# Four attention steps accumulate their output projection in two borrowed PSUM banks, the last Q products run ahead of one step, and a scratch tile changes its bank

## The chip, the cores and the metric

The kernel runs on one core of a Trainium2 chip. The metric is the device time of one execution in microseconds (us). Each timed execution also lists the mean granted clock of TensorE, the share of full speed that the chip let the matmul engine run at. All executions whose state is on record are "fast", so all may be compared.

Engines are named as the profile names them: PE is TensorE's matmuls, PEld its weight loads, DVE is VectorE, ACT is ScalarE, SPq a DMA queue. Times inside a profile count from the start of the profiled execution.

## The reference

One transformer block on x of shape 1 x 2048 x 1024, in bfloat16: layer normalisation, linear attention with 32 heads, a residual, layer normalisation, a gated MLP of width 3584, a residual.

```python
def _A_ref(x, wqkv, wo):                     # linear attention, 32 heads of 32
    q, k, v = ...                            # from x @ wqkv
    phi = lambda t: jnp.where(t > 0, t + 1, jnp.exp(t)) + 1e-6
    pq, pk = phi(q), phi(k)
    kv = jnp.einsum("bhsd,bhse->bhde", pk, v)
    z = jnp.einsum("bhsd->bhd", pk)
    num = jnp.einsum("bhqd,bhde->bhqe", pq, kv)
    den = jnp.einsum("bhqd,bhd->bhq", pq, z)[..., None] + 1e-6
    o = num / den
    return (...o...) @ wo                    # the output projection
# ... _B_ref: (relu(x @ W_gate) * (x @ W_up)) @ W_down
h = x + _A_ref(_layernorm(x), A_wqkv, A_wo)
h2 = h + _B_ref(_layernorm(h), B_W_gate, B_W_up, B_W_down)
```

## The kernel before

The large products (Q, K, V, gate, up, down) use a scheme of Strassen's kind. It needs sums of sub-blocks of the operands (`left_sums`) and recombines partial products. In the stretch that matters here, three streams share TensorE:

- the last Q products (`q_unit`, profile names Aq, Dq, Eq at line 437),
- the attention steps: numerator and denominator (nd), a DMA transpose (oT), the output projection (attn), and then the residual and second layer normalisation on ScalarE and VectorE,
- the first gate and up products of the MLP (Aq, Dq, Eq at line 693), which need the transposed normalised rows and their sums.

All accumulate in PSUM. In this stretch the pools hold two banks of tag A, two of tag E, one of tag D for the Strassen products, and three of tag ab for the attention steps.

```python
spin = pspool.tile([P, NW], FP32, tag="E", bufs=2, name="spin")   # scratch for matmuls at the very start
...
def nd():                                    # three tiles of tag "ab" in each step
    for c0, n in pieces:
        ps = ndpool.tile([P, NW], FP32, tag="ab", name="nd")
        for c in range(c0, c0 + n):
            nc.tensor.matmul(ps[...], lhsT=pqT[...], rhs=kvz[:, c, :], start=True, stop=True)
        # ... ScalarE: den = ln(...), rd = exp(-den)
        # ... VectorE: o_sb = numerator * rd        -> this frees the bank
def wo_h():                                  # two more tiles of tag "ab" in each step
    for j in range(2):
        ps = abpool.tile([P, NW], FP32, tag="ab", name="attn")
        for c in range(KC):                  # 8 matmuls of 128 x 512
            nc.tensor.matmul(ps[:], lhsT=st["oT"][:, c, :], rhs=wo_sb[...], start=(c == 0), stop=(c == KC - 1))
        nc.vector.scalar_tensor_tensor(...)  # x_res = attn + x_res, frees the bank
    # ... h to DRAM; LayerNorm: two passes over hn on ScalarE and small steps; the transpose of hn follows
...
LAG = (0, 1, 1, 2, 4)                        # nd, oT, x_in, wo_h, hn_T: steps after a tile begins
STS = 8; QSTEPS = 8
for step in range(QSTEPS):                   # steps 0..7: Q products between the attention steps
    attn_step(step)
    ...
    for p in rest[step * len(rest) // QSTEPS:(step + 1) * len(rest) // QSTEPS]:
        next(p)                              # one Q group
# steps 8..11: attention alone, with one gate/up unit; steps 12..19: with gate/up products between them
```

In the traces, a ScalarE or VectorE instruction waits for those queued ahead of it on its engine, even when its own input is ready. An example from the profile before: the step rd at 211.21 us follows a LayerNorm pass that runs from 210.08 to 211.22, though its input den was done at 210.18.

## Time and profile before

The three executions before the prediction took 747.36, 748.55 and 749.38 us; the profiled one took 748.8 us at a granted clock of 0.999.

The first line below is from the summary page of the profile: each engine's busy time (share of the span). The second is from its list of the costliest groups: line, engine, operation, operands, count, then busy us and mean ns, then idle time in front of them.

```profile
PE 725.9 (97%) x4020; PEld 382.2 (51%) x4020; DVE 568.4 (76%) x1023; ACT 324.6 (43%) x596; POOL 5.8 (1%) x44
L536 PE MATMUL attn<-wo_mem,oT 128*128 128x512 bf16 x256 | 57.8, 379 | 3.4 <-DVE o_sb L516 3.1
```

TensorE is the limit. The next view is the busy time of each engine by stretch. Its columns are the stretch, its length, then busy us and instruction count for PE, PEld, DVE, ACT and POOL, then the granted clock, the DMA share and GB/s.

```profile
198.00:230.00 32.00, 25.95 (x143) 12.36 (x142) 27.97 (x82) 22.41 (x66) 0.00 (x0) 1.00 0.71 168
260.00:300.00 40.00, 37.00 (x171) 16.54 (x170) 27.79 (x67) 21.30 (x42) 0.00 (x0) 1.00 0.43 131
300.00:700.00 400.00, 400.00 (x2241) 219.09 (x2239) 309.19 (x478) 128.96 (x172) 0.00 (x0) 1.00 0.64 213
```

From 300 us on PE has no idle time to give. Between 198 and 230 us it idles 6 of 32 us. The list of PE's waits from 185 to 300 us gives what it waited for: total us, number of times, longest. These are its five largest entries.

```profile
PE attn L536 <- DVE o_sb L516: 3.0, 6, 0.9
PE nd L509 <- DVE x_res L538: 1.9, 2, 1.3
PE Aq L693 <- ACT m L153: 1.8, 1, 1.8
PE nd L509 <- DVE pq_mem L201: 1.8, 1, 1.8
PE accA L773 <- DVE gu L702: 0.8, 1, 0.8
```

And these are rows of PE's timeline in that stretch: start, duration, what it is, and in brackets how long PE idled just before and what ended it.

```profile
187.59 3.61 PE L536 MATMUL attn<-wo_mem,oT 128*128 128x512 bf16 x16 [0.40 <-DVE o_sb L516]
...
203.83 0.23 PE L509 MATMUL nd<-kvz,pq_mem 128*128 128x132 bf16 x1 [1.79 <-DVE pq_mem L201]
204.97 3.61 PE L536 MATMUL attn<-wo_mem,oT 128*128 128x512 bf16 x16 [0.90 <-DVE o_sb L516]
...
210.52 3.61 PE L536 MATMUL attn<-wo_mem,oT 128*128 128x512 bf16 x16 [0.43 <-DVE o_sb L516]
...
215.85 3.61 PE L536 MATMUL attn<-wo_mem,oT 128*128 128x512 bf16 x16 [0.39 <-DVE o_sb L516]
...
221.12 0.28 PE L509 MATMUL nd<-kvz,pq_mem 128*128 128x132 bf16 x2 [1.28 <-DVE x_res L538]
222.05 3.61 PE L536 MATMUL attn<-wo_mem,oT 128*128 128x512 bf16 x16 [0.65 <-DVE o_sb L516]
...
262.93 3.62 PE L536 MATMUL attn<-wo_mem,oT 128*128 128x512 bf16 x16
...
297.49 1.02 PE L773 MATMUL accA<-hn,wg 128*128 128x512 bf16 x4 [0.78 <-DVE gu L702]
```

This is one rotation of three ab banks. A step takes five tiles from it, so each product waits until VectorE has emptied the tile of three turns before: projection behind o_sb, num/den behind x_res. The E banks are idle meanwhile: in PE's timeline no E product runs between the last of Q (198.45 us, 0.59 long) and the first of gate and up (232.18). The first row and the last two (the projections of steps 6 and 16, and the first accumulator of the feed-forward part, accA) serve as marks.

### The profile page before, as it was taken

How to read it: one execution, taken by the hardware profiler on the slowest of the kernel's cores; microseconds unless marked ns; L12 is line 12 of the kernel's file. 1: busy time of each engine (PE TensorE's matmuls, PEld its weight loads, DVE VectorE, ACT ScalarE, POOL GpSimd, SP SyncE). 2: the span in 40 equal slices, each digit the busy share in tenths (PEclk: the TensorE clock that was granted, in tenths of full speed). 3: DMA queues.
4: the chain of work that ended last, by engine and by line, in shares of the span. 5: the costliest groups of instructions: out<-in, count | busy, mean ns of one | idle time of the engine just before them, and what ended most of it. 6: DMA issues, size and time to landing. Idle time of an engine off the chain costs nothing.

```text
span 747.0 us, 10654 instructions
## 1 busy us (share of the span) xinstructions
PE 725.9 (97%) x4020; PEld 382.2 (51%) x4020; DVE 568.4 (76%) x1023; ACT 324.6 (43%) x596; POOL 5.8 (1%) x44
## 2 busy tenths in 40 slices
PE   7999999999889999999999999999999999999997
PEld 3444555444344444444444444444444458888666
DVE  6997644777886767678777788877787469996797
ACT  4876554778767645344444344343435220000000
POOL 0000000000000000000000000000000000000000
PEclk9999999999999999999999999999999999999999
DMA  9766002069777525164837349476574399988822
GB/s 317 159 145 154 1 1 94 20 146 249 170 173 172 134 79 183 39 182 121 237 127 207 125 140 317 149 211 212 183 261 149 101 388 361 317 284 299 306 79 79
DMA packets 146580, 132.03 MB, mean 177 GB/s; under 512 B 50913, under 2 KB 128097, under 8 KB 146529
## 3 DMA queue, kind: packets, MB, share of 16 engines
q1 hardware_dynamic: 135392, 123.23, 54.4%
q10 hardware_dynamic: 11136, 8.13, 3.4%
q8 instruction: 31, 0.51, 0.3%
q14 instruction: 21, 0.16, 0.1%
HBM read 79.95 MB, written 39.85 MB: 160 GB/s over the span
## 4 chain that ended last, share of the span: by engine, by line
PE 79%; DVE 8%; ACT 5%; DMA 5%; issue 1%; SPq 0%; POOL 0%; DVEq 0%; ACTq 0%
PE accA L773 22%; PE accY L773 8%; PE accX L773 8%; PE accA L1105 8%; PE attn L536 5%; PE Aq L297 3%; PE accA L934 3%; PE accX L1105 3%; PE Aq L437 3%; PE accY L1105 2%; DMA hn<-hn 2%; PE Aq L693 2%; PE Eq L297 2%; PE accX L934 2%; PE accY L934 2%
## 5 line engine op out<-in xcount | busy, mean ns | idle before, releaser
L783 ACT ACTIVATE gu<-gu 128x512 bf16<-128x512 bf16 x72 | 45.4, 630 | 131.9 <-DVE gu L782 127.4
L778 ACT COPY snap<-accA 128x1024 f32<-128x1024 f32 x72 | 72.4, 1008 | 37.0 <-PE accA L773 36.9
L536 PE MATMUL attn<-wo_mem,oT 128*128 128x512 bf16 x256 | 57.8, 379 | 3.4 <-DVE o_sb L516 3.1
L773 PEld LDWEIGHTS <-tg 128*128 128x128 f16 x384 | 37.6, 98 | 45.3
L773 PEld LDWEIGHTS <-tu 128*128 128x128 f16 x384 | 37.6, 98 | 45.3
L782 DVE TENSOR_TENSOR gu<-accY,snap 128x1024 bf16<-128x1024 f32 x36 | 43.9, 1219 | 9.7 <-ACT snap L778 9.7
L153 ACT COPY u<-Aq 128x512 f32<-128x512 f32 x56 | 32.2, 581 | 43.9 <-PE Aq L297 20.3
L782 DVE TENSOR_TENSOR gu<-accX,snap 128x1024 bf16<-128x1024 f32 x36 | 43.9, 1219 | 7.2 <-PE accX L773 4.7
L773 PE MATMUL accA<-hn,tg 128*128 128x512 f16 (+1 forms) x192 | 49.3, 379 | 0.0
L773 PE MATMUL accA<-hn,tu 128*128 128x512 f16 (+1 forms) x192 | 49.3, 379 | 0.0
L1105 PEld LDWEIGHTS <-x 128*128 128x128 f16 (+1 forms) x448 | 43.8, 98 | 5.5
L773 PEld LDWEIGHTS <-wg 128*128 128x128 bf16 x288 | 28.2, 98 | 34.9 <-issue 1.1
L773 PEld LDWEIGHTS <-wu 128*128 128x128 bf16 x288 | 28.2, 98 | 34.0
L536 PEld LDWEIGHTS <-oT 128*128 128x128 bf16 x256 | 25.0, 97 | 35.0 <-issue 6.7
L786 DVE TENSOR_TENSOR hq<-gu 128x512 bf16<-128x512 bf16 x48 | 20.3, 423 | 14.3 <-ACT gu L783 14.2
L297 PEld LDWEIGHTS <-xT 128*128 128x128 bf16 (+1 forms) x192 | 18.6, 98 | 24.5 <-issue 3.2
L516 DVE TENSOR_TENSOR o_sb<-nd,rd 128x384 bf16<-128x384 f32 (+1 forms) x48 | 22.8, 507 | 8.6 <-ACT rd L515 7.5
L1105 PEld LDWEIGHTS <-xs 128*128 128x128 f16 x280 | 27.4, 98 | 3.2
L538 DVE SCALAR_TENSOR_TENSOR x_res<-attn,x_res 128x512 bf16<-128x512 f32 x32 | 22.0, 688 | 6.3 <-PE attn L536 6.2
L934 PEld LDWEIGHTS <-x 128*128 128x128 bf16 (+1 forms) x168 | 16.5, 98 | 19.6
L1111 DVE TENSOR_TENSOR snap<-accA,u 128x1024 f32<-128x1024 f32 x16 | 19.5, 1220 | 8.3 <-PE accA L1105 8.1
L773 PE MATMUL accA<-hn,wg 128*128 128x512 bf16 x96 | 24.6, 379 | 0.8 <-DVE gu L702 0.8
(232 smaller groups left out, 1415.0 us busy)
## 6 DMA issues: line engine op xcount, KB each, us to landing
x<-x_dram SPq DMA_DIRECT2D x17, 896.0 KB, 8.2
x_dram<-hq SPq DMA_DIRECT2D x28, 512.0 KB, 3.0
wg<-in_B_W_gate_dram SPq DMA_DIRECT2D x14, 512.0 KB, 5.2
wu<-in_B_W_up_dram SPq DMA_DIRECT2D x14, 512.0 KB, 7.4
wraw<-in_B_W_down_dram SPq DMA_DIRECT2D x14, 512.0 KB, 4.9
x_dram<-hq SPq DMA_DIRECT2D x28, 256.0 KB, 2.6
t_dram<-wt SPq DMA_DIRECT2D x28, 256.0 KB, 2.2
xd<-x_dram SPq DMA_DIRECT2D x6, 896.0 KB, 7.2
```

What stands on the lines that cost most here:

```text
L153: nc.scalar.copy(out=snaps[nm, v], in_=A[v][:])
L297: nc.tensor.matmul(ps[:], lhsT=left[m - 1][:, kc, r + v * P:r + (v + 1) * P], rhs=right[m - 1][:, kc, :], start=(start and kc == 0), stop= ...
L437: nc.tensor.matmul(ps[:], lhsT=rq[m - 1][:, kc, (c + v) * P:(c + v + 1) * P], rhs=left[m - 1][:, kc, :], start=(start and kc == 0), stop=( ...
L516: nc.vector.tensor_tensor(out=ov[:, c0:c0 + n], in0=ndv[:, :, 0:P].rearrange("p k (h e) -> p k h e", h=HPC), in1=rd[:, 0:n, :].unsqueeze(3 ...
L536: nc.tensor.matmul(ps[:], lhsT=st["oT"][:, c, :], rhs=wo_sb[:, c, j * NW:(j + 1) * NW], start=(c == 0), stop=(c == KC - 1))
L538: nc.vector.scalar_tensor_tensor(out=h_sb[:, j * NW:(j + 1) * NW], in0=ps[:], scalar=1.0, in1=h_sb[:, j * NW:(j + 1) * NW], op0=ALU.mult, ...
L773: nc.tensor.matmul(ps[:, v, :], lhsT=w[v][n - 1][:, kc, :], rhs=left[n - 1][:, kc, :], start=(t is not None and kc == 0), stop=(kc == KH - ...
L778: nc.scalar.copy(out=st[nm][:], in_=halves(st["A"]))
L782: add(out=g[:], in0=halves(st[nm]), in1=st[base][:], op=ALU.add)
L783: nc.scalar.activation(out=g[:, 0, :], in_=g[:, 0, :], func=ACT.Relu)
L934: nc.tensor.matmul(ps[:, t * NW:(t + 1) * NW], lhsT=x_tile(n, s, kh)[:, f, (t0 + t) * P:(t0 + t + 1) * P], rhs=w_tile(n, kh)[:, f, :], sta ...
L1105: nc.tensor.matmul(pv[:, tt, :], lhsT=left(m)[:, f, tt * P:(tt + 1) * P], rhs=right(m)[:, f, :], start=(t is not None and f == 0 and tt % ...
```

## The change

The intent is to let the projection of steps 8 to 11 accumulate in the two idle E banks, so that num/den keeps the three ab banks for itself. For that the E banks have to be free by then, so the last Q products go ahead of step 7. Thirdly the scratch tile of the very first matmuls moves from tag E to tag A. The author's reading is that this makes A the first tag used, so that the pool gives A the first banks and the feed-forward's first accumulator overlays A's banks and not E's. The traces name no banks. What they show is accA's wait on gu: 0.78 us before.

```diff
-            spin = pspool.tile([P, NW], FP32, tag="E", bufs=2, name="spin")
+            spin = pspool.tile([P, NW], FP32, tag="A", bufs=2, name="spin")
...
-        def wo_h():
+        def wo_h(borrow):
...
-                ps = abpool.tile([P, NW], FP32, tag="ab", name="attn")
+                if borrow:
+                    ps = pspool.tile([P, NW], FP32, tag="E", bufs=2, name="attn")
+                else:
+                    ps = abpool.tile([P, NW], FP32, tag="ab", name="attn")
...
-                stages[n][k]()
+                if k == 3:
+                    stages[n][k](QSTEPS <= step < STS + LAG[-1])
+                else:
+                    stages[n][k]()
...
     for step in range(QSTEPS):
+        now = rest[step * len(rest) // QSTEPS:(step + 1) * len(rest) // QSTEPS]
+        if step == QSTEPS - 1:
+            while now:
+                next(now.pop(0))
         attn_step(step)
...
-        for p in rest[step * len(rest) // QSTEPS:(step + 1) * len(rest) // QSTEPS]:
+        for p in now:
             next(p)
```

In `attn_step`, k == 3 is the projection. No arithmetic is added or removed.

## The prediction

> **What bounds the kernel now.** TensorE. The page gives PE 725.9 us of a 747.0 us span (97%) at a granted clock of 0.999. The busy time by stretch shows PE busy throughout from 300 us on, so the feed-forward part has nothing to give. PE idles in the first 20 us (4.3), at 40 to 80 us (2.4) and between 198 and 297 us (about 10), where this change works.
>
> **The place.** In the timeline of PE from 198.9 us (end of the last Q product) to 228 us (first product that needs the sums of normalised rows) I count 6.2 us of idle: 1.79 (released by the phi of Q), 0.90, 0.43, 0.39, 1.28, 0.65, 0.59 and small ones. The list of waits names them: the projection on o_sb (3.1 us, 7 times), num/den on x_res (1.9 us, 2). That is one PSUM rotation of three banks: a step takes three num/den tiles and two projection tiles from it, so each waits until VectorE drains the other. The two E banks are unused meanwhile. [...]
>
> **What changes.** No arithmetic is added or removed; PE keeps its instruction count, 3.46 us of projection a step included. (1) The instruction order shows the projection in E in four steps, interleaved with num/den. (2) Before that, the last four Q groups (3.5 us) run ahead of step 7's num/den and projection, so E is free in time. (3) Two D products of the gate/up quad (0.87 us each), which filled holes at 209 and 214 us, come later; moved, not lost. (4) The spin tile takes tag A, so A gets the first banks; the feed-forward's first accumulator then lies on A's banks, not E's. Its wait at 297 us on the last gu from E (0.78 us) should vanish.
>
> **Costing.** Placing the new order by hand with durations from the trace (x_res 0.61, o_sb 0.46, hn 1.15 twice plus 0.9 of small ScalarE operations, transposes 3.1 to 3.5 to landing), the PE row that stood at 228.7 us comes at about 222.7: 6 us earlier. VectorE becomes the next limit: it was busy 18.9 of 20 us from 200 to 220, and ScalarE is in order, LayerNorm's passes ahead of den/rd. About 0.8 us returns as a new wait of the projection at 229 us; I allow 1.5 us more for semaphores, queueing and late oT transposes. Kept: about 4 us, plus 0.7 at 297. Everything after is PE-bound, so it reaches the end.
>
> **Prediction: 744.0 us** (before 748.55), 8 in 10 between 741.8 and 747.0. Faster by over 2%: 0.01; within 2%: 0.98; slower by over 2%: 0.01.
>
> **What would show it.** Busy time by stretch: PE from 200 to 230 us loses most of its 6 us of idle. Waits: projection on o_sb below 1.5 us, num/den on x_res gone or smaller, accA on gu gone. PE's busy total stays within 1 us. The 300 us boundary arrives 4 to 5 us sooner; the length after it is unchanged. The wait near 270 us (1.8 us, ScalarE behind a LayerNorm) stays.
>
> **What would make it wrong.** If VectorE and ScalarE order, not banks, paces the four steps, num/den waits replace the old ones and the gain is 1 to 2 us. If step 7's later num/den delays its transpose, PE waits for oT near 205 us. If the wait at 270 us grows, part is given back; if it vanishes, the gain is near 6.5.

6 us less 0.8 and 1.5 is 3.7, taken as about 4, and with the 0.7 that is 4.4 to 4.7 us off 748.55, put at 744.0. Two of its statements can be read in the profile before. The 16 matmuls of a projection take 3.45 us from their start to that of the next product (204.97 to 208.42). ScalarE in order, with LayerNorm's passes ahead of rd, is seen at 211.21: rd, ready at 210.18, follows the pass that runs from 210.08 to 211.22.

## The result, and the profile after

The changed kernel is correct. Its four first executions took 743.43, 744.81, 743.89 and 742.76 us, the median 743.66; the kernel before (the three executions above and one more) had a median of 748.43. The ratio is 0.9938, with a 95% interval of 0.9918 to 0.9957. In this document a ratio is the mean time of one kernel's fast runs over that of the other's in the same rounds, so not quite the ratio of the medians quoted. Six more executions gave a median of 743.42. They were run at other times.

The same lines of the profile after, from its page:

```profile
PE 721.8 (97%) x3967; PEld 382.2 (52%) x4020; DVE 567.7 (77%) x1023; ACT 324.4 (44%) x596; POOL 6.0 (1%) x44
L539 PE MATMUL attn<-wo_mem,oT 128*128 128x512 bf16 x246 | 58.1, 379 | 4.6 <-DVE o_sb L516 2.5
```

PE's busy time seems to have fallen by 4.1 us, but the trace holds only 3967 matmul records, 53 fewer than before, while the weight loads are 4020 in both, with the same 382.2 us. The change removes no matmul, so the busy totals of PE can't be compared to the microsecond here. The same holds between 300 and 700 us below, where 24 records fewer go with 1.4 us less of busy time. The gaps between records with a named releaser are the safer reading.

Busy time by stretch after:

```profile
198.00:230.00 32.00, 28.76 (x165) 14.22 (x165) 28.30 (x84) 26.86 (x82) 0.51 (x1) 1.00 0.92 218
260.00:300.00 40.00, 37.62 (x172) 17.04 (x174) 28.16 (x67) 19.71 (x37) 0.00 (x0) 1.00 0.44 132
300.00:700.00 400.00, 398.63 (x2217) 219.23 (x2241) 309.71 (x475) 127.15 (x169) 0.00 (x0) 1.00 0.65 216
```

PE's waits from 185 to 300 us after, the three largest:

```profile
PE attn L539 <- DVE o_sb L516: 2.3, 4, 1.3
PE Aq L703 <- ACT m L153: 1.8, 1, 1.8
PE attn L539 <- DMA oT<-o_sb: 1.5, 2, 1.3
```

The waits of num/den on x_res and on phi of Q (pq_mem) are gone, and so is the wait of accA. What is left in PE's timeline is in few places:

```profile
187.24 3.61 PE L539 MATMUL attn<-wo_mem,oT 128*128 128x512 bf16 x15 [0.39 <-DVE o_sb L516]
...
199.45 3.61 PE L539 MATMUL attn<-wo_mem,oT 128*128 128x512 bf16 x16 [0.36 <-DVE o_sb L516]
...
214.56 1.25 PE L539 MATMUL attn<-wo_mem,oT 128*128 128x512 bf16 x5 [1.27 <-DMA oT<-o_sb]
...
221.02 3.61 PE L539 MATMUL attn<-wo_mem,oT 128*128 128x512 bf16 x16 [1.31 <-DVE o_sb L516]
...
258.50 3.62 PE L539 MATMUL attn<-wo_mem,oT 128*128 128x512 bf16 x16
...
292.12 1.03 PE L783 MATMUL accA<-hn,wg 128*128 128x512 bf16 x4
```

Three points of the two timelines tell where the time came from. The projection of step 6 starts at 187.59 us before and 187.24 after, so little has happened until then. The projection of step 16 starts at 262.93 and 258.50: from step 6 it takes 75.34 us before and 71.26 after, 4.1 us less. The accumulator accA starts at 297.49 and 292.12, which adds 0.9 us. From there to the end it takes 449.51 and 449.48 us. All but 0.4 us of the 5.4 us between the two profiles is therefore gained in the 110 us between step 6 and accA, as planned. Two single profiles are good for this to about a microsecond only: step 6 itself starts at 186.25 us in one other profile (d1), without anything changed before it.

### The profile page after: what moved, and what is told of

The parts are those of the page before. It is cut to its first block, busy times and chain, and to the rows that moved or that the text cites. A ratio compares the mean times of both kernels' runs of the same rounds, so it can differ in the third digit from the quotient of the medians.

```text
span 741.6 us, 10606 instructions
## 1 busy us (share of the span) xinstructions
PE 721.8 (97%) x3967; PEld 382.2 (52%) x4020; DVE 567.7 (77%) x1023; ACT 324.4 (44%) x596; POOL 6.0 (1%) x44
## 4 chain that ended last, share of the span: by engine, by line
PE 78%; DVE 8%; ACT 5%; DMA 5%; issue 1%; SPq 0%; POOL 0%; DVEq 0%; ACTq 0%
PE accA L783 22%; PE accX L783 8%; PE accY L783 8%; PE accA L1115 8%; PE attn L539 4%; PE Aq L297 3%; PE accA L944 3%; PE accX L1115 3%; PE Aq L437 2%; PE accY L1115 2%; DMA hn<-hn 2%; PE Eq L297 2%; PE accY L944 2%; PE Aq L703 2%; PE accX L944 2%
## 5 line engine op out<-in xcount | busy, mean ns | idle before, releaser
L199 ACT ACTIVATE e<-pq_mem,negb 128x512 bf16<-128x512 bf16 x32 | 22.5, 717 | 5.4 <-DVE pq_mem L194 5.2
```

Of the source, the lines that this page charges most:

```text
L199: nc.scalar.activation(out=e, in_=dst, func=ACT.Exp, bias=negb[:, 0:1], scale=1.0)
```

## The experiments

The first theory was the prediction's: the holes are the ab rotation's, borrowed banks remove them, the Q products ahead only make the banks free, and the bank order is worth the 0.8 us wait of accA. The rival: the order of work on VectorE and ScalarE paces the stretch, so that borrowing alone moves the holes and Q-ahead is a change in its own right. Twelve runs were made in four calls, each call on another chip and each run with five rounds beside the kernel before (a2, a4 and b4 have five executions, the others six). All were correct. A second cause came into view, the granted clock; the last four experiments are for it.

One table for all, so that the runs can be compared. "Below 0.999" counts the executions whose mean granted clock was under 0.999. The last column is worked out from each profile and is explained in the section on the clock.

| kernel | median us (range) | ratio to before, same rounds | below 0.999 | poorest 3.41 us: PE work |
|---|---|---|---|---|
| before, 44 runs beside | 748.71 (746.65–752.05) | 1 | 26 of 44 | 0.72 |
| after (first four, then c0) | 743.66; 743.42 (742.75–744.52) | 0.9938; 0.9924 [0.9908, 0.9941] | 0 of 10 | 1.59; 1.54 |
| a1, borrowing only | 747.17 (746.52–749.56) | 0.9984 [0.9971, 0.9997] | 6 of 6 | 0.95 |
| a2, Q ahead only | 749.01 (748.57–749.37) | 1.0006 [0.9994, 1.0017] | 3 of 5 | 1.27 |
| a3, bank order only | 746.83 (746.67–750.04) | 0.9985 [0.9971, 1.0] | 2 of 6 | 0.72 |
| a4, all but the bank order | 745.48 (744.37–746.22) | 0.9958 [0.9945, 0.9971] | 2 of 5 | 1.56 |
| b1, five steps borrow | 742.02 (740.49–745.54) | 0.9904 [0.9879, 0.9929] | 2 of 6 | 1.29 |
| b2, two steps borrow | 749.30 (745.10–750.66) | 0.9993 [0.9969, 1.0016] | 5 of 6 | 0.00 |
| d3, b2 again | 748.48 (747.25–749.80) | 0.9997 [0.9975, 1.0019] | 6 of 6 | 0.00 |
| b4, b1 with late sums | 741.70 (741.00–742.21) | 0.9896 [0.9879, 0.9914] | 0 of 5 | 1.87 |
| d1, before with idle matmuls | 749.75 (748.78–753.33) | 1.0026 [1.0002, 1.005] | 4 of 6 | 0.92 |
| d2, b2 with idle matmuls | 746.94 (746.59–749.31) | 0.9986 [0.9965, 1.0008] | 1 of 6 | 1.60 |
| d4, d1 with late sums | 750.47 (749.41–753.37) | 1.0032 [1.0011, 1.0052] | 5 of 6 | 1.00 |

### The parts of the change alone

**a1: borrowing only** (scratch tile in E, Q products in their old place).

```diff
 # against the changed kernel
-            spin = pspool.tile([P, NW], FP32, tag="A", bufs=2, name="spin")
+            spin = pspool.tile([P, NW], FP32, tag="E", bufs=2, name="spin")
...
-        if step == QSTEPS - 1:
-            while now:
-                next(now.pop(0))
```

> Only the borrowing of the two E banks in four steps; Q products and bank order as before. Theory 1 (the shared rotation of three banks made the holes): most of the gain of the stretch is here, 2.5 to 3.5 us of the 4.8, so about 745.5 us; the waits of the projection on o_sb fall from 3.0 to under 1.5 us. Rival 2 (the gain comes from running the last Q products, and so phi, earlier): under 1 us. The accA wait of 0.8 us at the start of the feed-forward part stays in either.

Measured: 747.17 us, 0.16% less than before. The large waits near 204 us went, but PE's timeline shows two new ones, on VectorE's work, 15 us later:

```profile
219.19 1.07 PE L509 MATMUL nd<-kvz,pq_mem 128*128 128x132 bf16 x8 [1.67 <-DVE o_sb L516]
...
221.60 1.01 PE L700 MATMUL Eq<-hs,tg 128*128 128x512 f16 x2 [1.33 <-DVE hs L117]
```

All six executions had a lowered clock, the unprofiled ones 0.997. Against those executions of the kernel before in the same rounds that were also below 0.999 (median 749.23) it is 2.2 us faster (747.03 at 0.997). So borrowing has a gain of its own, smaller than first expected, and it trades the bank waits for waits on VectorE's o_sb and the sums (hs).

**a2: Q ahead only.**

```diff
 # against the changed kernel, with the scratch tile in E
-                    stages[n][k](QSTEPS <= step < STS + LAG[-1])
+                    stages[n][k](False)
```

> Only the last four Q groups ahead of step 7; projection in its old banks, bank order as before. Theory 1: it takes away the 1.8 us hole that num/den has behind phi, but the rotation still makes holes, so 0.5 to 1.5 us gained, about 747.4 us, and the waits of the projection on o_sb plus num/den on x_res stay near 4 us. Rival 2: 3 us or more, under 745.5 us.

Measured: 749.01 us, the same as before or slower, where a gain of 0.5 to 1.5 us was expected. (Its two executions at full clock, 749.01 and 749.24, are 1.3 us above the full-clock median of before in these rounds, 747.83; two are too few to build on.) The projections still wait on o_sb (4.2 us, 6 times, the longest 2.08) and num/den on x_res (1.9 us). Taking the Q products away from that stretch without other banks leaves PE with less to do there. So Q-ahead is no gain of its own; it only helps together with borrowing. Together they gain more than the sum: 2.2 us and nothing alone (each compared as said), 3.3 us as a pair (a4, below).

**a3: bank order only**, the one line of the scratch tile.

> Only the spin tile's tag, that is the order in which the banks are given out. My reading: the accA wait on gu (0.78 us) disappears and nothing else moves, 0.8 us gained, about 747.6 us. Rival 3: the bank order is without effect of its own, 748.4 us, and the wait moves to the next accumulator (accX).

Measured: the wait of accA, 0.78 us before, is gone from the list of waits, and at full clock the four executions (746.67 to 746.87) have a median 1.06 us below the full-clock executions of the kernel before in the same rounds (747.83). Its profiled execution shows the same holes as before, with a lowered clock behind them; more on it below.

**a4: the whole change but the scratch tile.** Its order of PE's instructions is that of the changed kernel.

> The whole change but the spin tile's tag. The instruction order on PE is the same as with it, so only the banks differ. My reading: the accA wait of about 0.8 us is back and the rest stays, about 744.5 us. Rival 3: as the whole change, 743.7 us.

Measured: 745.48 us. The wait of accA is back in its profile:

```profile
PE accA L783 <- DVE gu L712: 0.8, 1, 0.8
```

The profile also has a wait of num/den on o_sb, 1.80 us at 218.31, which both profiles of the changed kernel lack although PE has the same order there; b4 below comes back to it. Its three executions at full clock have a median of 744.56, 3.27 us under the 747.83 of before. At full clock the two parts thus add up to 1.06 + 3.27 = 4.3 us, against 3.8 measured for the whole change (747.21 to 743.42); the terms are no better known than to about half a microsecond.

**c0: the changed kernel again**, on the chip of the next experiments.

> The changed kernel unaltered, to have it beside the others on one chip with more timed runs. My reading: as measured, 743.7 us, 4.7 under before. Second question, which the partial versions raised: executions of the kernel before fall into two groups, about 747.8 us at a granted clock of 1.000 and about 749.3 at 0.997 to 0.998. If the holes on PE bring the lower clock on, the changed kernel, with fewer holes, should show it in fewer executions than 6 of 11; if it is chance alone, in about as many.

Measured: 743.42 us, ratio 0.9924, and no execution below 0.999.

### How many steps should borrow

**b1: a fifth step borrows.** The longest wait left after, 1.31 us at 221.02, is the projection of step 12. It is the first one back in the ab banks and waits until VectorE has emptied the first num/den tile of its own step.

```diff
-                    stages[n][k](QSTEPS <= step < STS + LAG[-1])
+                    stages[n][k](QSTEPS <= step < STS + LAG[-1] + 1)
```

> The change, with a fifth step borrowed. In the profile after the change the first step that goes back to the shared banks waits 1.31 us for the drain of the first num/den tile. Theory 1 (shared rotation): that wait goes, 0.6 to 1.3 us under the changed kernel, about 742.7 us. Rival 4 (by then the latency chain of LayerNorm, transpose and sums paces it): the wait only moves to the first product that needs the sums, no gain.

Measured: 742.02 us. The wait at step 12's projection is gone, and the wait on ScalarE's m near 268 us fell from 1.82 to 0.65. Two of its six executions have a lowered clock. At full clock the medians are 740.99 (four executions) against 743.42 for the changed kernel (c0, six), and the two groups do not overlap. In the profiled execution num/den waited 2.12 us on o_sb at 219.50 instead, with a lowered clock after it:

```profile
219.50 0.34 PE L509 MATMUL nd<-kvz,pq_mem 128*128 128x132 bf16 x3 [2.12 <-DVE o_sb L516]
```

**b2: only the first two steps borrow** (`- 2` in place of `+ 1`).

> The change, with only the first two of the four steps borrowed. Theory 1: the holes of the last two steps return (0.65, 1.28, 0.59 us and small ones in the profile before), so 1 to 2 us over the changed kernel, about 745.3 us. Rival 5 (only the first steps count, since PE then runs ahead into the latency chain anyway): within 0.5 us of the changed kernel.

Measured: 749.30 us, no better than before, although two steps do borrow. Both expectations, 745.3 us and about the time of the changed kernel, failed. The first step back in ab now waits 3.84 us, and then its 16 matmuls take 6.37 us, where the same 16 take 3.61 at full clock:

```profile
215.27 0.28 PE L509 MATMUL nd<-kvz,pq_mem 128*128 128x132 bf16 x2
219.39 6.37 PE L539 MATMUL attn<-wo_mem,oT 128*128 128x512 bf16 x16 [3.84 <-DVE o_sb L516]
```

So the hole moved to where borrowing stops, and a second cost came with it.

**b4: b1, with the sums of the second half's rows issued after the step's other work.**

```diff
 # against b1
                 if k == len(LAG) - 1 and n % STS >= NT:
-                    left_sums(hnT[n // STS], hns[n // STS], ..., nc.vector)
+                    if n // STS:
+                        late.append(n)              # issued at the end of the step
+                    else:
+                        left_sums(hnT[n // STS], hns[n // STS], ..., nc.vector)
```

> The fifth step borrowed, and the operand sums of the second half issued after the step's other work instead of at its start, so that VectorE does not stand waiting for a transpose ahead of the projection's evacuation. The wait near 267 us (1.8 us, the snap behind a LayerNorm on ScalarE) should fall under 0.7 us; together with the fifth step about 2 us under the changed kernel, near 741.7 us. If the wait stays, its cause is not that order.

Measured: 741.70 us, the fastest median of all, 1% below before and below the changed kernel too, with no execution below 0.999. Whether the late sums did it is not shown: at full clock b1 is as fast (four executions, median 741.0), and the wait on m had already shrunk in b1. What b4 had in its favour is that its profile lacks the 2.12 us hole of b1; there the transpose of hn, on which VectorE stood, was followed by VectorE's work at 215.77 and not at 217.42 us. The traces show one step more: this transpose was issued at 212.06 us in b4 and at 212.10 in b1, but landed 3.7 us after its issue in b4 and 5.3 us in b1. The late sums hardly explain that: the same transpose took 5.1 us in a4 (the 1.80 us wait noted there) and 3.6 and 3.7 in the two profiles of the changed kernel, whose PE order is that of a4. What makes it land late is not shown.

### The clock

Two groups of executions stand apart in the kernel before. The 18 of 44 at 0.999 or more have a median of 747.48 us (746.65 to 748.05), the 26 below a median of 749.27 (748.26 to 752.05). In a profile the clock can be read by stretch. These are 1 us stretches of a3's profile, behind its two holes of 1.78 and 0.90 us (columns as above; the granted clock is the third number from the right):

```profile
201.00:202.00 1.00, 0.00 (x0) 0.00 (x0) 1.00 (x5) 1.00 (x7) 0.00 (x0) 1.00 0.87 225
202.00:203.00 1.00, 0.23 (x1) 0.11 (x2) 1.00 (x4) 1.00 (x3) 0.00 (x0) 1.00 0.44 168
203.00:204.00 1.00, 0.24 (x1) 0.10 (x1) 1.00 (x4) 0.92 (x5) 0.00 (x0) 0.83 0.00 0
204.00:205.00 1.00, 1.00 (x4) 0.30 (x3) 1.00 (x3) 0.33 (x1) 0.00 (x0) 0.50 0.58 104
...
206.00:207.00 1.00, 1.00 (x4) 0.29 (x2) 0.00 (x0) 0.00 (x0) 0.00 (x0) 0.50 0.93 198
207.00:208.00 1.00, 1.00 (x6) 0.42 (x5) 0.69 (x3) 0.00 (x0) 0.00 (x0) 0.96 1.06 195
```

The clock falls to 0.50 at 203.66 and returns at 207.07: 3.41 us. I located the falls between 185 and 300 us in all profiles: there are eleven, in a1 (two), a2, a3, b1, b2 (two), d1, d3 (two) and d4. Eight last 3.41 us (to 0.01) and three twice that, 6.83. In the 3.41 us before each of them PE was busy for only 0.79 to 1.46 us. One such fall is half a clock for 3.41 of 747 us, 0.0023 of the mean clock, which is what separates 0.998 from 1.0; and by estimate it costs up to 1.7 us, half of 3.41, where PE has work (in a3 the projection behind the fall took 5.24 us in place of 3.61). A mean of 0.999 needs no fall in this stretch: in the profile of before the clock is at 0.50 only for the last 1.1 us of the span, after PE's last matmul, where it costs nothing.

The depth (0.50) and the lengths (3.41 and 6.83 us) are what the traces show. What sets them, and why a hole is followed by a fall in one execution and not in another, is not shown: the profile of before has the same two holes as a3's (1.79 and 0.90), and its clock did not fall.

As a description I summed PE's busy time over every stretch of 3.41 us, the length of a fall, between 186 and 285 us of a profile. Its least value is the column "poorest 3.41 us". In the nine rows where it is 1.29 us or less, at least two of the executions were below 0.999 (2 of 6 in a3 and b1, all six in a1 and d3). In the four kernels where it is 1.54 or more, after had 0 of 10, b4 0 of 5, d2 1 of 6 and a4 2 of 5. So little PE work and falls go together, but the amount does not say how often: 0.72 us goes with 26 of 44 in before and with 2 of 6 in a3, and a4 with 1.56 had falls where c0 with 1.54 had none. Besides, one profile stands for executions that differ. The next four runs test whether holes cause the falls.

**d2: b2, with twelve matmuls of no use put into its 3.84 us hole**, and **d3: b2 again beside it.** They write to a tile that nobody reads, so the result stays correct.

```diff
+            if warm:                             # step 11 only
+                idle = pspool.tile([P, NW], FP32, tag="E", bufs=2, name="idle")
+                for _ in range(12):
+                    nc.tensor.matmul(idle[:], lhsT=st["oT"][:, 0, :], rhs=wo_sb[:, 0, 0:NW], start=True, stop=True)
```

> The kernel with two borrowed steps, plus twelve matmuls of no use (estimate 2.6 us) in the hole of 3.84 us before the projection of step 11. Clock theory: most executions at a mean clock of at least 0.999, where five of six of the kernel with two borrowed steps were at 0.992 to 0.995, and the time falls by 2 to 5 us, to 744.5 to 747.5 us. Rival (the dip is not due to the hole): clock as low as there, and the time 749 to 751 us. If the twelve themselves delay work: clock high and the time 747 to 749.

> The kernel with two borrowed steps once more, on the same chip and in the same rounds as its filled twin. Clock theory: most executions at a mean clock of 0.992 to 0.995 and 748.5 to 750.7 us; chance: a share of dips unlike the first time.

Measured: d3 was below 0.999 in six of six executions, d2 in one of six. The kernel with twelve matmuls more has the lower median, 746.94 against 748.48 us, but their ranges overlap (746.59 to 749.31 and 747.25 to 749.80), so the time alone would prove little with six executions each; the count of lowered clocks is what separates them. The difference of 1.5 us is under the 2 to 5 that was expected, though the time itself is in the expected range, since d3 was faster than b2's first call. In d2's timeline the same projection waits 1.81 us and then runs at full speed, 3.61 us; in d3 it takes 6.34. The first two lines are d2's, the third is d3's:

```profile
214.75 2.10 PE L535 MATMUL idle<-wo_mem,oT 128*128 128x512 bf16 x9
218.66 3.61 PE L543 MATMUL attn<-wo_mem,oT 128*128 128x512 bf16 x16 [1.81 <-DVE o_sb L516]
...
219.62 6.34 PE L539 MATMUL attn<-wo_mem,oT 128*128 128x512 bf16 x16 [3.67 <-DVE o_sb L516]
```

This is the cleanest comparison: the filler does nothing but keep PE busy, and the clock stayed up. Here the hole causes the fall. (The wait on m near 270 us, behind which d3's profile has a second fall, shrank too, from 2.39 to 1.60 us, so not all of the count is due to the filled hole itself.) That the shorter holes of the kernel before cause its falls in the same way is argued from this and from the eleven falls; d1 and d4, which were to test it, do not decide it.

**d1: the kernel before, with four such matmuls in each of the steps 8 to 11.**

> The kernel before, with four matmuls of no use (estimate 0.9 us from 0.22 us each) per step in steps 8 to 11, written to the unused E bank in the place where the engine stands idle. Clock theory (holes close together make the granted clock dip for about 3 us): fewer of its executions are below a mean clock of 0.999 than the 14 of 22 of the kernel before, and its time is no longer than before, 746.5 to 748.5 us, although it does 16 more matmuls. Rival (the dips come by chance or from the chip, not from the holes): as many dips as the kernel before in the same rounds, and the time is the same or longer by up to 2 us.

Measured: the number that the clock theory gave failed: four of six below 0.999, and 749.75 us, slower than before by 0.26%. The profile shows why the count did not drop. The fills did their work where they stood: the poorest 3.41 us near 201 us rose from 0.72 to 2.61 us of PE work and near 219 from 1.48 to 2.82. But at 270 us the wait for ScalarE's m became longer, 2.50 us against 1.82 before, and the one fall of the profile came there, at 270.93:

```profile
270.41 1.39 PE L704 MATMUL Aq<-hs,tu 128*128 128x512 f16 x4 [2.50 <-ACT m L153]
```

PE had come to this point 0.74 us sooner, counted from step 6, but ScalarE's copy of m had not (it came 0.07 us sooner), so the gain was handed back as a wait. That would account for the falls that remain; the two executions at full clock are still 1.8 us slower than before's.

**d4: d1 with the late sums of b4**, meant to shorten that wait and so to leave at most one of six executions with a lowered clock.

> The kernel before, with the idle matmuls of d1 in steps 8 to 11 and the sums of the second half's normalised rows after the step's other work (as in b4). Reading so far: the clock falls for 3.41 us at a time, and in the ten falls that the profiles show the 3.41 us before the fall had the engine busy for 0.8 to 1.46 us. In d1 the fills lifted the poorest 3.41 us near 201 us from 0.72 to 2.61 us of work and near 219 from 1.48 to 2.82, but the one near 268 fell from 1.58 to 0.92, and there the clock fell. Clock theory: with the late sums the wait near 268 us is below 1.5 us, no 3.41 us of the profile have less than 1.6 us of work, and at most 1 of 6 executions is below a mean clock of 0.999; time 746.5 to 748.5 us, 1.5 to 3 us below d1. Rival (dips come by chance): 3 or more of 6 below 0.999, as before. Third outcome: a new hole elsewhere, seen in the profile.

Measured: the third outcome, a hole where it should not be. The wait at 270 us stayed at 2.41 us, the fall of the clock came at 271.29, behind it, and five of six executions were below 0.999. Late sums alone do not shorten the wait on m; in b1 it was short without them. The run doesn't tell the theories apart, but it does not speak against the holes as the cause either.

## Why the prediction was right or wrong

The prediction was 744.0 us, and the change gave 743.66 and 743.42. Point by point:

1. **"What bounds the kernel now. TensorE."** Right. From accA to the end nothing changed (449.51 and 449.48 us), and every microsecond won before that reached the end.
2. **"That is one PSUM rotation of three banks".** Right as to the mechanism: with E borrowed and Q moved, the waits on x_res (1.9 us) and pq_mem (1.8 us) are gone. The runs add that neither part does it alone (a1 0.9984, a2 1.0006, both together 0.9958).
3. **"6 us earlier", less "0.8 us" and "1.5 us more": "Kept: about 4 us".** Right in size for the profiled pair: step 6 to step 16 took 4.1 us less. The allowance was needed: 1.27 us for the transpose oT at 214.56, and 0.36 and 0.19 in small holes. The 1.27 us end with the transpose, whose input, the third piece of o_sb, comes late because its reciprocal on ScalarE is queued behind LayerNorm passes: its num/den product was done at 206.21, ScalarE ran passes at 206.84 and 207.98 and took its den at 209.12, VectorE wrote the piece at 210.00, and the transpose was issued at 210.48. I saw this order in the trace; no run tests it.
4. **"About 0.8 us returns as a new wait of the projection at 229 us".** Wrong in size, and in place if 229 is a time of the changed kernel. It was 1.31 us at 221.02, at the projection of step 12, the first that does not borrow; near 229 only 0.24 us is left, at 230.73. (Step 12 stood at 228.08 us in the profile before; the prediction does not say which timeline it means.) I had looked for where VectorE gets short and overlooked that the bank rotation bites again at the very step where borrowing ends. b1 and b2 show it: extending the borrowing by a step removes the wait, cutting it by two makes it 3.84 us. This was the mis-sized term, and mending it is worth 1.4 us in medians (743.42 to 742.02) and 2.4 at full clock (743.42 to 740.99).
5. **"plus 0.7 at 297".** Right: the wait of 0.78 us vanished, and a3 alone gives 1.06 us at full clock.
6. **"The wait near 270 us (1.8 us ...) stays."** Right: 1.82 before, 1.82 after.
7. **"projection on o_sb below 1.5 us"**: wrong, 2.3 us, for the reason of point 4. **"PE's busy total stays within 1 us"** can't be judged, because of the missing records.
8. **The clock.** The prediction quotes "a granted clock of 0.999" and carries no term for it. It subtracted from 748.55, the median of three executions, of which two most likely were of the group with falls, going by their times alone (these three list no clock, and the profiled execution took 748.8 at 0.999, so a time is no proof). Over all rounds before's mean is 748.65 us and after's (ten executions) 743.68, a gain of 5.0. Of that, 3.8 us is the difference at full clock (747.45 to 743.68 in means) and 1.2 us is by how much the falls raise the mean of before. In ten executions the changed kernel had none; its profiles have no 3.41 us with less than about 1.54 us of PE work, but a4, with 1.56, had falls in two of five, so this reason is argued and not shown. So the total was close to the forecast partly by luck, because two errors offset each other: at full clock the change gave 3.8 us and not the 4.6 predicted, and the clock gave 1.2 that were not predicted.

What stays open: how little PE work it takes for the clock to fall, and why it does so only in some executions, the 1.27 us wait for oT, what b4's late sums do by themselves, why the transpose of hn lands late in some profiles, why the profiled pair shows 5.0 us between step 6 and accA where the means at full clock differ by 3.8 (the profile of before, 748.8 us without a fall, is itself longer than all 18 full-clock executions, 746.65 to 748.05), and the 1.8 us that d1 lost at full clock.

## What to carry to other kernels

When banks are borrowed to break a rotation, look at the first tile that goes back to the old rotation, because the wait gathered there (1.31 us after the change, 3.84 in b2); and look at whether the borrowed banks are free early enough, since half of such a change may be worth nothing (Q ahead alone had a ratio of 1.0006). Read the granted clock of every execution beside its time: idle stretches of TensorE of two to three microseconds in sum (2.12 in b1, 1.78 and 0.90 in a3), even broken up by small matmuls, were followed by half a clock for 3.41 us, and only in some executions, so a median of three may mix two groups. Before filling holes on one engine, check that the next wait on the path is not set by another engine, or the gain is handed back there (in d1 PE came 0.74 us sooner and waited 2.50 us for ScalarE in place of 1.82).
